# A convolution, scan and out-projection kernel on one core: five tiles per stream to begin with, masked taps on GpSimd, spare quarters on two banks

## The chip, the cores and the metric

The kernel runs on one core of a Trainium2 chip. The metric is the device time of one execution in microseconds, lower is better. Each execution that was profiled also has a span, from its first to its last instruction, which is 1.7 us shorter than its time (346.14 against 344.4). Below, "the trace" means the profiled execution, and "timed" all executions that a run lists. The profiled one is among these, except in the first run of before, where it took 346.14 us and is not among the four. No run is marked as in the chip's slower state (the single execution of before_look has no mark); "slow" below means longer than others of the same kernel.

## The reference, cut to what matters

```python
# x (8, 4224, 192), weight (8, 7): a causal convolution with one softmaxed row of 7 taps per head of 24 columns
out = np.einsum('hk,bskhg->bshg', w, x_unf)
# then a gated linear recurrence of 512 channels and a projection back to 192
proj = x @ w_in
val, gate = (proj[..., :D_inner], proj[..., D_inner:])
for t in range(S):
    h = a[0, 0] * h + val[:, t, :]
    ys[:, t, :] = h
silu = gate * (1.0 / (1.0 + np.exp(-gate)))
return (silu * ys @ w_out).astype(np.float32)
```

The rows of the eight sequences are taken as two streams of 16896. A stream is cut into tiles of 112 rows for the convolution and into 33 blocks of 512 for the rest. With four groups of 128 channels that makes 132 steps.

## The kernel before

TensorE (PE) does the convolution as matmuls with a banded matrix of taps (`tb`), transposes, projects, and projects back. A step is one `phase` (8 matmuls of 512 columns: the values of the next step, the gates of this one), two scans on VectorE (DVE), two silus on ScalarE (ACT), a product silu x scan on GpSimd (POOL), a part of the convolution of a later group, and two or three quarters of the out-projection. A quarter is 4 matmuls of 192 columns; two quarters fill half an output tile (a block of one stream), one PSUM bank, which ACT copies out. The 256 quarters are eight more than two for each of the 124 steps that take them; these eight are the "spare" ones.

```python
    def seam_taps(t):                      # where a tile holds the end of one sequence and the start of the next
        off = seams[t]
        if t not in tbs:
            tbs[t] = singles.tile([K, H, M], BF16, name=f"tb_{t}")
            nc.scalar.copy(tbs[t], tb)
        else:
            nc.scalar.memzero(tbs[t][0 : off + HB, :, off:M])
    # ... cut ...
            for k in range(2):             # of outp(): w counts the output tiles, k their halves
                ps = bank(k if w >= WL else 0)
                for b in (2 * k, 2 * k + 1):
                    outp_mm(ps, w, b, range(NC))
                    # ... cut: ACT copies after the second quarter, a store after the fourth ...
    # ... cut ...
    F = QT + QT // 2                       # six tiles of each stream are loaded, convolved and turned first
    # ... cut ...
    phase(-1)                              # the first projection
    second(FQ, QT, bank(0), bank(1), (nc.scalar, nc.scalar))   # what is left of the second four tiles
    WL = NOUT - 8
    for s in range(NSTEP):
        # ... cut: scan, phase, product, loads ...
        if 0 < gr <= len(seams) and o < 2:
            seam_taps(sorted(seams)[gr - 1])
        for k, n in enumerate(todo.get(s, [])):
            conv(n, 1 - k)                 # convolutions of later groups, on bank 1, until step 119
        if s >= 2 * LW:
            for _ in range(3 if s >= NSTEP - SPG and s % 2 == 0 or s == NSTEP - 1 else 2):
                next(out_quarters)
```

## Time and profile before

| | before |
|---|---|
| time, median of 4 runs (range) | 344.57 us (344.29 to 344.79) |
| time of the profiled execution | 346.14 us, span 344.4 us |
| PE, DVE, POOL, ACT busy | 96%, 94%, 90%, 74% |
| idle of PE behind the bank's copy | 4.9 us in 5 waits |

These are the busy shares of its page and two rows of its costliest groups (busy us, mean ns of one, then idle time of the engine before them and what ended most of it):

```profile
PE 329.0 (96%) x2605; PEld 179.1 (52%) x2608; DVE 324.4 (94%) x312; ACT 256.4 (74%) x525; POOL 309.9 (90%) x177
...
L425 PE MATMUL pm<-wout,y 128*128 128x192 bf16 x1040 | 107.3, 246 | 5.1 <-ACT osb L457 4.9
...
L255 ACT COPY tb<-tb 128x896 bf16<-128x896 bf16 x3 | 2.8, 940 | 0.0
```

The row of line 425 is the out-projection; its 5.1 us of idle PE are what the third part of the change aims at. Line 255 is the copy of the taps that the second part moves. The rows of a timeline further down give start and length in us, then engine, line, operation, tiles, shapes and count; a bracket holds the idle time of the engine before the row and what ended it.

### The profile page before, as it was taken

To read this page: it belongs to the slowest core of one execution; us is meant where nothing else is said; L and a number is where in the kernel's file an instruction comes from. 1 tells how busy PE (TensorE), PEld (TensorE's weight loads), DVE (VectorE), ACT (ScalarE), POOL (GpSimd) and SP (SyncE) were. 2 spreads that over 40 slices of the span, in tenths; PEclk is the share of its full clock that TensorE was granted. 3 is DMA by queue.
4 is the path that set the end of the run, shared out by engine and by line. 5 is a ranking of instruction groups with operands and counts; after the bars stand their busy time and mean duration, and the time that the engine had idled before them with its cause. 6 is when DMAs were issued, how large, how long until landed. Compare 5 with 4: busy or idle time off the path is not lost.

```text
span 344.4 us, 7246 instructions
## 1 busy us (share of the span) xinstructions
PE 329.0 (96%) x2605; PEld 179.1 (52%) x2608; DVE 324.4 (94%) x312; ACT 256.4 (74%) x525; POOL 309.9 (90%) x177
## 2 busy tenths in 40 slices
PE   6989999999999999999999999999999999969993
PEld 2533545555555555555555555555555555535553
DVE  4799999999999999999999999999999999967993
ACT  5777878778788887777877878777877877755662
POOL 8779999898999899989998999999999999856991
PEclk9999999999999999999999999999999999999998
DMA  8996999999799989978996999797969594442225
GB/s 152 159 135 99 148 184 200 200 144 187 141 196 143 212 141 188 161 192 133 191 166 191 149 195 177 170 133 193 158 190 147 137 176 131 104 116 93 91 93 185
DMA packets 124878, 54.28 MB, mean 158 GB/s; under 512 B 90758, under 2 KB 124522, under 8 KB 124842
## 3 DMA queue, kind: packets, MB, share of 16 engines
q1 hardware_dynamic: 85034, 38.21, 49.3%
q0 software_dynamic: 39424, 15.24, 40.4%
q8 instruction: 20, 0.33, 0.4%
q10 hardware_dynamic: 384, 0.37, 0.4%
q14 instruction: 16, 0.13, 0.2%
HBM read 31.04 MB, written 25.95 MB: 165 GB/s over the span
## 4 chain that ended last, share of the span: by engine, by line
PE 86%; DMA 5%; ACT 3%; DVE 3%; issue 2%; POOL 0%; DVEq 0%; ACTq 0%; POOLq 0%
PE pm L425 25%; PE pv L342 15%; PE pg L342 15%; PE pg L350 11%; PE pm L282 11%; PE pv L350 8%; DMA out_dram<-osb 3%; DVE h L396 2%; DMA xb<-in_x_dram 2%; ACT sg L378 1%; ACT osb L457 1%; ACT tb L255 0%; PE pg L425 0%; POOL xb L126 0%; ACT xc L527 0%
## 5 line engine op out<-in xcount | busy, mean ns | idle before, releaser
L396 DVE TENSOR_TENSOR_SCAN h<-av,h,pv 128x512 bf16<-128x512 f32 (+3 forms) x256 | 293.9, 1209 | 7.0 <-POOL y L414 4.7
L414 POOL TENSOR_TENSOR y<-sg,h 128x1024 bf16<-128x1024 bf16 x130 | 274.2, 2123 | 25.6 <-ACT sg L378 22.0
L378 ACT ACTIVATE sg<-pg 128x512 bf16<-128x512 f32 x262 | 142.2, 595 | 72.6 <-PE pg L350 68.4
L425 PE MATMUL pm<-wout,y 128*128 128x192 bf16 x1040 | 107.3, 246 | 5.1 <-ACT osb L457 4.9
L425 PEld LDWEIGHTS <-y 128*128 128x128 bf16 x1056 | 84.8, 98 | 17.3 <-issue 16.4
L342 PE MATMUL pv<-xc,w 128*128 128x512 bf16 x265 | 79.7, 379 | 1.6 <-DVE h L396 1.3
L342 PE MATMUL pg<-xc,w 128*128 128x512 bf16 x260 | 77.8, 379 | 0.6 <-ACT sg L378 0.4
L342 PEld LDWEIGHTS <-w 128*128 128x128 bf16 x528 | 49.3, 98 | 33.9 <-issue 3.8
L457 ACT COPY osb<-pm 128x384 f32<-128x384 f32 x128 | 63.4, 499 | 1.9 <-DMA out_dram<-osb 0.9
L282 PEld LDWEIGHTS <-tb 128*112 128x112 bf16 x438 | 33.2, 129 | 45.5 <-issue 45.3
L350 PE MATMUL pg<-xc,w 64*128 64x512 bf16 x262 | 51.0, 386 | 0.0
L350 PE MATMUL pv<-xc,w 64*128 64x512 bf16 x266 | 50.6, 376 | 0.0
L282 PE MATMUL pm<-xb,tb 128*112 128x192 bf16 (+7 forms) x419 | 48.7, 238 | 0.0
L350 PEld LDWEIGHTS <-w 64*128 64x128 bf16 x528 | 15.3, 94 | 57.0 <-issue 56.8
L112 ACT CAST ymain<-pm 112x512 bf16<-112x512 f32 x73 | 42.6, 589 | 0.4 <-PE pm L282 0.4
L126 POOL DMA_DIRECT2D xb<-in_x_dram x30 | 29.7, 1006 | 0.8 <-POOLq L614 0.8
L396 DVE TENSOR_TENSOR_SCAN h<-av,pv 128x512 bf16<-128x512 f32 (+3 forms) x32 | 25.2, 798 | 0.8 <-PE pv L350 0.8
L303 ACT CAST yquad<-pm 112x512 bf16<-112x512 f32 x36 | 21.2, 589 | 0.0
L176 PE MATMUL pg<-wm 128*128 128x512 bf16 x11 | 5.1, 629 | 1.7 <-DVE wm L169 1.7
L176 PEld LDWEIGHTS <-wm 128*128 128x128 bf16 x14 | 1.5, 127 | 3.8 <-issue 1.9
L114 DVE CAST ymain<-pg 112x512 bf16<-112x512 f32 x1 | 0.7, 690 | 2.3 <-PE pg L282 2.3
L255 ACT COPY tb<-tb 128x896 bf16<-128x896 bf16 x3 | 2.8, 940 | 0.0
(70 smaller groups left out, 39.6 us busy)
## 6 DMA issues: line engine op xcount, KB each, us to landing
out_dram<-osb SPq DMA_DIRECT2D x65, 384.0 KB, 3.0
xb<-in_x_dram POOLq DMA_DIRECT2D x12, 768.0 KB, 8.8
xb<-in_x_dram POOLq DMA_DIRECT2D x9, 384.0 KB, 9.7
xc<-ymain SPq DMA_TRANSPOSE x70, 4.1
xb<-in_x_dram POOLq DMA_DIRECT2D x4, 192.0 KB, 6.6
xc<-yquad SPq DMA_TRANSPOSE x35, 3.2
xraw<-in_x_dram SPq DMA_DIRECT2D x2, 192.0 KB, 4.3
xb<-in_x_dram POOLq DMA_DIRECT2D x2, 144.0 KB, 5.9
```

The source lines that it names most:

```text
L112: eng.copy(o, i)
L126: eng.dma_start(t[:, b0:n, :], dataclasses.replace(xf, offset=xf.offset + (row + b0 * M) * D, ap=[[D, K], [M * D, n - b0], [1, D]],),)
L176: nc.tensor.matmul(ps, wm[:, 0:P], wm, start=True, stop=True)
L282: nc.tensor.matmul(pc[:, :, t0 - a0 : t1 - a0, lo - lo0 : hi - lo0], tap[:, h, :], xbs[g][:, :, a + t0 : a + t1, lo:hi], start=(lo == lo0) ...
L303: nc.scalar.copy(y.rearrange("p t d -> p (t d)"), ps[0:M, :])
L342: nc.tensor.matmul(ps[st], w1[:, m * P : (m + 1) * P], xc[:, st, t], start=True, stop=False)
L350: nc.tensor.matmul(ps[st], w2[r, m * P : (m + 1) * P], xc[r, 2, t], start=False, stop=True)
L378: nc.scalar.activation(sg[:, st * N : st * N + N], pgs[st], Act.Silu)
L396: nc.vector.tensor_tensor_scan(h[:, o + lo : o + hi], av[:, c : c + 1].to_broadcast([P, hi - lo]), pv[st][:, lo:hi], initial=0.0 if lo in ...
L414: eng.tensor_mul(y, sg, h)
L425: nc.tensor.matmul(bank[:, b % 2 * D : b % 2 * D + D], y[:, b : N : NB] if w >= NOUT - 2 else y[:, b * P : b * P + P], wout[:, c, :], star ...
L457: nc.scalar.copy(osb[:, 2 * k : 2 * k + 2, :].rearrange("p b d -> p (b d)"), ps[:, 0 : 2 * D],)
```

## The change

Its intent is in three parts. (1) Begin with five tiles of each stream instead of six, so that the first projection has less to wait for. (2) Make the three masked copies of the taps on GpSimd before its first product, instead of on ACT in the middle of the steps. (3) Spread the eight spare quarters of the out-projection so that none comes while convolutions still hold bank 1, and alternate the banks from then on.

```diff
-    F = QT + QT // 2
-    assert F * M >= N
+    F = -(-N // M)
+    assert F == QT + 1
...
-    def seam_taps(t):
-        ... (cut, shown above)
+    for t, off in seams.items():
+        tbs[t] = singles.tile([K, H, M], BF16, name=f"tb_{t}")
+        nc.gpsimd.tensor_copy(tbs[t], tb)
+        nc.gpsimd.memset(tbs[t][0 : off + HB, :, off:M], 0.0)
...
-    second(0, FQ, p1[0], p2[0], (nc.vector, nc.scalar))
+    second(p1[0], 0, 1, 0, D1, nc.vector)
+    second(p2[0], 0, 1, D1, D, nc.scalar)
...
     phase(-1)
-    second(FQ, QT, bank(0), bank(1), (nc.scalar, nc.scalar))
+    second(ps_g.tile([P, N], FP32, name="pg_0"), 1, QT, D1, D, nc.scalar)
+    for k in range(2):
+        second(bank(k), 1, QT, k * D2R, k * D2R + D2R, nc.scalar)
     out_quarters = outp()
-    WL = NOUT - 8
+    WL = NOUT - 10
+    spare = [NSTEP - 12 + 2 * k for k in range(6)] + [NSTEP - 3, NSTEP - 1]
...
-        if 0 < gr <= len(seams) and o < 2:
-            seam_taps(sorted(seams)[gr - 1])
...
-            for _ in range(3 if s >= NSTEP - SPG and s % 2 == 0 or s == NSTEP - 1 else 2):
+            for _ in range(3 if s in spare else 2):
```

The body of `second` is rewritten for one piece at a time (cut here).

More of the change, by code (lines that the diff above doesn't have):

```diff
@@ L248 @@
     tbs = {}
-    def seam_taps(t):
-        off = seams[t]
-        if t not in tbs:
-            tbs[t] = singles.tile([K, H, M], BF16, name=f"tb_{t}")
-            nc.scalar.copy(tbs[t], tb)
-        else:
-            nc.scalar.memzero(tbs[t][0 : off + HB, :, off:M])
+    for t, off in seams.items():
+        tbs[t] = singles.tile([K, H, M], BF16, name=f"tb_{t}")
+        nc.gpsimd.tensor_copy(tbs[t], tb)
+        nc.gpsimd.memset(tbs[t][0 : off + HB, :, off:M], 0.0)
     one = singles.tile([NC, NC], FP32, name="one")
@@ L476 @@
     p2 = [ps_v.tile([P, n], FP32, name=f"pv_{k}") for k, n in enumerate((N, NC))]
-    tiles = lambda p, d: p[0:M, :].rearrange("p (s a d) -> p s a d", d=d, s=2)
     mixed = lambda p: p[0:M, :].rearrange("p (a s d) -> p s a d", s=2, a=QT)
@@ L483, with second @@
     nc.scalar.copy(ymix[0][:, 0:QT, :], p1[1][0:M, :].rearrange("p (t d) -> p t d", d=P))
-    FQ = F - QT
-    def second(a0, a1, pa, pb, eng):
-        taps(tiles(pa, P), 1, 0, P, a0, a1)
-        taps(mixed(pb)[:, :, a0:a1, :], 1, D1, D, a0, a1)
-        copy(eng[0], y1[:, :, a0:a1, :], tiles(pa, P))
-        copy(
-            eng[1], ymix[0][:, QT + a0 : QT + a1, :],
-            pb[0:M, :].rearrange("p (t d) -> p t d", d=P)[:, a0:a1, :],
-        )
-    second(0, FQ, p1[0], p2[0], (nc.vector, nc.scalar))
+    m1 = ymix[0].rearrange("p t (s d) -> p s t d", s=2)[:, :, QT : HT, :]
+    def second(ps, a0, a1, lo, hi, eng):
+        pc = ps[0:M, 0 : 2 * (a1 - a0) * (hi - lo)].rearrange(
+            "p (s a d) -> p s a d", s=2, a=a1 - a0
+        )
+        taps(pc, 1, lo, hi, a0, a1)
+        to = m1[:, :, a0:a1, :] if lo == D1 else y1[:, :, a0:a1, lo:hi]
+        copy(eng, to, pc)
+    second(p1[0], 0, 1, 0, D1, nc.vector)
+    second(p2[0], 0, 1, D1, D, nc.scalar)
     av = singles.tile([P, NC], FP32, name="av")
```

## The prediction

> **What bounds the kernel now.** I read the page's busy shares first. TensorE (PE) is busy 96% of 344.4 us, VectorE (DVE) 94%, GpSimd (POOL) 90%, ScalarE (ACT) 74%. So I did not look for a busy engine but for the idle time of PE, and asked for PE's waits stretch by stretch. Of the whole span after the start:
>
> ```profile
> PE pm L425 <- ACT osb L457: 4.9, 5, 1.2
> PE pv L342 <- DVE h L396: 1.3, 5, 0.4
> ```
>
> (us in total, times, the longest.) Line 425 is the out-projection, line 457 the copy that empties its PSUM bank, line 396 the scan. Of the first row the last 45 us alone hold:
>
> ```profile
> PE pm L425 <- ACT osb L457: 3.9, 4, 1.2
> ```
>
> The timeline of that stretch shows the four:
>
> ```profile
> 302.46 0.49 PE L425 MATMUL pm<-wout,y 128*128 128x192 bf16 x4 [0.82 <-ACT osb L457]
> ...
> 306.22 0.49 PE L425 MATMUL pm<-wout,y 128*128 128x192 bf16 x4 [1.18 <-ACT osb L457]
> ...
> 309.78 0.82 PE L425 MATMUL pm<-wout,y 128*128 128x192 bf16 x8 [1.23 <-ACT osb L457]
> ...
> 315.55 0.49 PE L425 MATMUL pm<-wout,y 128*128 128x192 bf16 x4 [0.62 <-ACT osb L457]
> ```
>
> Each is a step where a quarter starts a new half tile while the one bank (pm_0) still waits for ACT, which does two silus (1.08 us) before the copy. Last, the chain that ended last, for the start:
>
> ```profile
> 1.32 0.95 POOL xb L126
> 2.27 5.80 DMA xb<-in_x_dram
> 8.21 0.65 PE pg L282 x7
> ...
> 11.87 0.59 PE pv L342 x2
> 12.46 0.44 PE pv L350 x2
> ...
> 23.55 1.55 DVE h L396 x2
> ```
>
> Three regimes follow. To 12.8 us the chain is load, convolution, transposes, first projection. From 12.8 to 33 us it is the scans: single scans start 1.171 us apart, so 2.34 us a step. From 33 us on it is PE: 2.42 us in a step with a convolution, 2.17 without (out-projection at 84.40 to 86.61, 151.87 to 154.04), and from 52.3 to 300.8 PE is busy 248.40 of 248.50 us. There only an idle PE can be won. Its waits after 33.2 us are one of 1.10 at 52.24, two of 0.05 at 86.61 and 120.19, and the four above.
>
> **What the Trainium skill says.** "PSUM — Partial Sum Buffer", Summary: rules for kernel authors, says to read PSUM while matmuls run from a different bank than the one written. The trace agrees: where quarters already alternate (after 317 us) no such wait is left. "GPSIMD Engine Reference", 3.1 Elementwise, gives about 2.6 cycles an element with two inputs, and 4.1 Engine selection says one input is roughly line rate. The trace agrees on the first: 1024 elements take 2.12 us, 2.07 ns each, some 2.5 cycles of the page's 1.2 GHz. No GpSimd copy is in this trace to test the second. "DMA: Bandwidth & Descriptors", Issuing engines are not separate DMA queues, says that all issuers share the same 16 engines and interleave. The trace agrees: output stores land 3.0 us after issue in the median, but the first, issued at 41.15 among loads and transposes, took 10.46.
>
> **Part 1: five tiles instead of six.** The raw float loads shrink from two tiles to one per stream (tile 0 comes apart), 512 packets of 768 B to 256. Until 6.5 us they share the engines with the GpSimd loads that the chain waits for. At about 50 ns a packet, as both kinds show, 256 packets over 16 engines are 0.8 us; I count 0.6 us off the landing at 8.07. The first transposes fall from 18 to 15 (0.058 us apart), the ACT copy of 672 columns (0.72 us) becomes one of 560 (about 0.62), the two DVE copies of 0.50 become about 0.44: together 0.2 us before the first projection. So the first scan starts about 0.8 us earlier, at 12.0.
>
> Part of that is paid back. What is left of the second quad is three tiles, not two: three ACT copies of 384 columns (0.50 each by the row of osb) in place of 0.58 and 0.38, nine transposes in place of six, and a DVE copy of 1008 columns in place of 672 (0.51, about 0.68). The transposes wait for the third ACT copy, so scan 1 comes about 0.45 us later after scan 0 than now. The DVE has 0.8 us of gaps before scans 2 and 3 (0.26 and 0.55), set by the chain of PE and ACT, which itself moves by some 0.3. Net at scan 3: 0.8 - 0.3 = 0.5 us earlier, and the scans then run back to back as now.
>
> **Part 2: masked taps on GpSimd.** ACT loses three copies of 128x896 (0.94 us each) and three zeroings (0.31 to 0.51): 4.05 us of ACT, but in the chain only where PE waits after them, at 86.61 and 120.19: 0.05 us each, 0.10 in all. At 52.24 ACT had finished its copy (49.82 to 50.76) and then waited 0.95 us for a store, so nothing is won there. GpSimd gains three copies and three memsets behind its ten load issues, which end at 13.5 us. Estimate from the skill's line rate and 1.2 GHz: 896 elements 0.75 us plus about 0.1 (its 1-element memset takes 0.10), up to 1.4 if slower; memsets of 256, 512 and 768 elements at the 1 ns an element of the 112-element memset (0.21 us), 0.3 to 0.9. Sum about 4.8 us, so the first product starts at 18.4 instead of 15.9. But GpSimd idles 1.78 us before the second product (19.79), and that one comes at about 20.5: a lag of 0.7 us that lasts while GpSimd is back to back, to about 53 us. Products have slack: that of step 3 ends at 26.9, its reader runs at 34.8; six buffers hold the silus. It costs nothing by itself, but the four loads of the third group (30.98 to 40.07) go out 0.7 us later.
>
> **Part 3: spare quarters.** The old spare quarter at step 118 (300.98) shifts the pairing and gives the waits at steps 118, 119, 120 and 122. Now steps 118 and 119, the last with convolutions on bank 1, take two quarters; from step 120 banks alternate, and of the 8 spare quarters 6 fall on even steps and 2 on steps 129 and 131. No step touches a bank twice across a copy. All four waits go: 0.82 + 1.18 + 1.23 + 0.62 = 3.85 us. PE has the same matmuls otherwise. Could DVE take over? Steps 119 to 129 hold 26.1 us of PE work by the pieces of the chain (1.40 a phase, 0.77 or 1.10 of quarters, 0.36 of convolution), 2.37 a step, against 2.34 for two scans: PE still sets it, barely. Its products hold: that of step 127 ends 4.8 us after the phase of 127 begins (phase 1.40, silu 1.2, product 2.2), and its first reader, the second quarter of step 129, comes some 6.4 us after (steps of 2.17 and 2.50, a phase of 1.40, one quarter of 0.33).
>
> **The join at 52 us.** Between the start and the PE regime lies the wait of 1.10 us, for a store that landed at 51.61. If its landing is fixed by the DMA traffic, arriving 0.5 us earlier only waits longer, and loads issued 0.7 us later may push it back. I give 3 in 4 that it stays, with PE resuming about 0.2 us later than now, and 1 in 4 that it vanishes and both it and the start's 0.5 are won: 0.75 x 0.2 - 0.25 x 1.6 = -0.25 us.
>
> Sum: -3.85 - 0.10 - 0.25 = -4.2 us, 344.4 to 340.2 us.
>
> **Rivals.** (a) The GpSimd work delays products and loads: if copies run at the two-input rate (1.9 us each, sum 8 us), the lag is near 3 us, the store at 52 lands later, and the total is about 342. For it: GpSimd has no idle time from 20 to 53 us; against it: products have over 7 us of slack. (b) The scan takes the place of the removed waits: DVE stood 4.69 us idle in the same stretch, so it has what it needs; if it were behind by a pair it would return at most 1 us: 341.2. (c) The store at 52 us lands early and the whole start counts: 344.4 - 3.85 - 0.1 - 1.1 - 0.5 to 1.0, 338.4 to 338.9. (d) The start gains nothing, as the load's last packets sit behind the projection weights' 2 KB packets: with the join holding, no change to the total.
>
> **Range and chances.** The end is counted from four measured waits, so the spread is nearly all that of the join, -1.6 to +1.2 us. 8 in 10: 338.9 to 341.6. Over 2% faster needs under about 337.6, more than all gains together: 4%. Slower by 2% would need a new stall of over 10 us: 1%.
>
> **What would show it.** In the changed profile: no wait of PE for line 457 after 300 us; quarters three to a step on 128 to 131; the first convolution near 7.6 and the first scan near 12.0 us; GpSimd copies from about 13.6 us, with the first product near 18.4; a single wait of PE near 52 us, of 1 to 2.3 us. Wrong would be: waits of scans for GpSimd, silus waiting for products, or gaps of PE behind the scan from step 120 on.

## More of the kernel before

Differences of the whole kernel are given between times, differences inside it between traces, and the two are not mixed without saying so.

Before the first convolution PE runs "warming" matmuls on zeros, `warm(pw, WARM)` with 7 and `warm(pw, WARM2)` with 4, as its clock begins at half speed: the first of them, of 512 columns, start 0.43 us apart, and matmuls of this size after the rise of the clock 0.22.

## The result, and the profile after

The changed kernel took 340.2 us in the median of 4 runs (339.2 to 341.54), before 344.57. The ratio is 0.9876, with a 95% interval of 0.9841 to 0.9911: 1.2% faster. A ratio is the mean time of one kernel's fast runs over that of the other's of the same rounds, so it is not quite the ratio of the medians that are quoted.

The page after, the rows that answer to those of before (the lines are renumbered: 421 is the old 425, 453 the old 457, 338 and 346 the old 342 and 350):

```profile
PE 327.9 (97%) x2608; PEld 178.9 (53%) x2609; DVE 323.7 (96%) x312; ACT 253.3 (75%) x520; POOL 313.8 (93%) x183
...
L421 PE MATMUL pm<-wout,y 128*128 128x192 bf16 x1040 | 106.7, 246 | 0.0
...
L253 POOL COPY tb<-tb 128x896 bf16<-128x896 bf16 x3 | 2.9, 952 | 0.0
```

The out-projection has no idle time left before it, and GpSimd has the copies. All waits of PE in the changed kernel (us in total, times, longest):

```profile
PE pg L176 <- DVE wm L169: 1.7, 1, 1.7
PE pv L338 <- DVE h L392: 1.3, 5, 0.4
PE pg L338 <- ACT sg L374: 0.4, 1, 0.4
PE pm L278 <- DMA xb<-in_x_dram: 0.3, 1, 0.3
PE pv L338 <- ACT xc L112: 0.2, 1, 0.2
```

The row "PE pm <- ACT osb" of 4.9 us is gone, and all that is left lies before 32 us. The timeline of PE at steps 119 to 121, where there had been waits of about a microsecond:

```profile
300.68 0.82 PE L421 MATMUL pm<-wout,y 128*128 128x192 bf16 x8
...
302.83 1.17 PE L421 MATMUL pm<-wout,y 128*128 128x192 bf16 x12
...
305.33 0.83 PE L421 MATMUL pm<-wout,y 128*128 128x192 bf16 x8
```

Rows of 8, 12 and 8 matmuls without a bracket: two, three and two quarters, with no wait before or within. The start of the chain that ended last:

```profile
5.63 2.27 POOL xb L126 x3
7.89 6.21 DMA xb<-in_x_dram
14.24 0.65 PE pm L278 x7
```

The chain of before waited at 8.21 us for the first loads. This one goes back, from the third group of four tiles at 14.24, to loads that GpSimd issued until 7.89: the beginning has moved in front of its data. And GpSimd's masks, by the timeline:

```profile
13.56 1.01 POOL L253 COPY tb<-tb 128x896 bf16<-128x896 bf16 x1
14.62 0.31 POOL L254 MEMSET tb<- 96x256 bf16 x1
...
17.31 0.73 POOL L254 MEMSET tb<- 32x768 bf16 x1
18.01 2.11 POOL L410 TENSOR_TENSOR y<-sg,h 128x1024 bf16<-128x1024 bf16 x1
```

They take from 13.56 to 18.01, 4.45 us, and the first product follows at once.

Between the two traces the scans run 1.20 us earlier from step 3 on, 2.56 us from step 52 on, and the last matmul ends 7.01 us earlier (339.20 and 332.19). The timed medians differ by only 4.4. The rest is the choice of executions: that of before was 1.6 us slower than its median, that of after 1.0 faster.

### The profile page after: what moved, and what is told of

It reads as the page before. It is cut to its first block, busy times and chain, and to the rows that moved or that the text cites. A ratio compares the mean times of both kernels' runs of the same rounds, so it can differ in the third digit from the quotient of the medians.

```text
span 337.5 us, 7251 instructions
## 1 busy us (share of the span) xinstructions
PE 327.9 (97%) x2608; PEld 178.9 (53%) x2609; DVE 323.7 (96%) x312; ACT 253.3 (75%) x520; POOL 313.8 (93%) x183
## 4 chain that ended last, share of the span: by engine, by line
PE 90%; DVE 3%; POOL 2%; DMA 2%; issue 1%; ACT 1%; DVEq 0%; POOLq 0%
PE pm L421 26%; PE pg L338 16%; PE pv L338 16%; PE pg L346 12%; PE pm L278 11%; PE pv L346 8%; DVE h L392 2%; DMA xb<-in_x_dram 2%; POOL xb L126 1%; PE pg L421 0%; ACT sg L374 0%; ACT xc L522 0%; DVE osb L114 0%; POOL w L202 0%; POOL w L201 0%
## 5 line engine op out<-in xcount | busy, mean ns | idle before, releaser
L278 PE MATMUL pm<-xb,tb 128*112 128x192 bf16 (+6 forms) x417 | 48.5, 238 | 0.3 <-DMA xb<-in_x_dram 0.3
L112 ACT CAST ymain<-pm 112x512 bf16<-112x512 f32 (+1 forms) x74 | 42.9, 586 | 0.5 <-PE pm L278 0.5
L253 POOL COPY tb<-tb 128x896 bf16<-128x896 bf16 x3 | 2.9, 952 | 0.0
L414 POOL TENSOR_TENSOR y<-sg,h 128x512 bf16<-128x512 bf16 x2 | 2.3, 1149 | 0.0
```

What stands on the lines that cost most here:

```text
L112: eng.copy(o, i)
L278: nc.tensor.matmul(pc[:, :, t0 - a0 : t1 - a0, lo - lo0 : hi - lo0], tap[:, h, :], xbs[g][:, :, a + t0 : a + t1, lo:hi], start=(lo == lo0) ...
```

## The experiments

**The change once more (again).** No edit.

> The changed kernel once more, as the yardstick for the three runs beside it. Its four earlier times lay between 339.2 and 341.54 us, against 344.29 to 344.79 of before, and its profile came from the fastest of them, while the profile of before came from an execution of 346.14. Theory: the times spread because the wait near 52 us for a store comes and goes; then the new trace shows either no wait of PE there and about 339 us, or one of 1 to 2 us and about 340.5. Rival: the spread is the granted clock (0.995 in the slowest, 0.999 in the fastest); then slow and fast executions differ by a lower clock in their records and not by a wait at 52 us.

Measured: 339.70 us (339.58 to 339.86), before 344.20, ratio 0.9864. The trace has no wait of PE after 33 us, and its profiled execution took 339.86, as the timed ones. Its first convolution began at 7.19 us, that of the first trace of after at 6.65: neither the wait at 52 us nor a lower clock later on makes the difference (in both, the clock falls only after the last matmul), but the start: scan 3 is at 20.62 instead of 20.11 and the last matmul ends 0.50 us later. More on that below.

**Without part 3 (no_part3).**

```diff
-    WL = NOUT - 10
-    spare = [NSTEP - 12 + 2 * k for k in range(6)] + [NSTEP - 3, NSTEP - 1]
+    WL = NOUT - 8
...
-            for _ in range(3 if s in spare else 2):
+            for _ in range(3 if s >= NSTEP - SPG and s % 2 == 0 or s == NSTEP - 1 else 2):
```

> The changed kernel with the old spare quarters and the old switch to two banks (part 3 undone). Theory: each of the four waits costs its shown idle time and besides the 0.16 us by which the last matmul before it is drawn longer (0.246) than matmuls follow one another (0.083): 3.85 + 4 x 0.16 = 4.5 us slower than the unchanged after of this round. Prediction as on record: 3.85 us. Rival: the scans would have limited the end anyway; then under 3.5 us.

Measured: 343.85 us, 4.15 slower than the change beside it. Nearly all of the gain sits here. (The two pieces of part 3, the steps of the spare quarters and the earlier use of two banks, were not run apart.) PE's waits from 290 us on, and two of the four in its timeline:

```profile
PE pm L421 <- ACT osb L453: 3.6, 4, 1.2
```

```profile
299.28 0.25 PE L421 MATMUL pm<-wout,y 128*128 128x192 bf16 x1
300.36 0.49 PE L421 MATMUL pm<-wout,y 128*128 128x192 bf16 x4 [0.83 <-ACT osb L453]
...
302.44 0.49 PE L421 MATMUL pm<-wout,y 128*128 128x192 bf16 x4
304.12 0.49 PE L421 MATMUL pm<-wout,y 128*128 128x192 bf16 x4 [1.18 <-ACT osb L453]
```

Here the true cost of a wait can be read. Four matmuls are drawn as 0.49 us from 302.44, but where matmuls follow on, the next begins 0.33 us after the first of the four. The last one is drawn 0.246 us long, while the next would have started after 0.083. So between the start of the last one and the next start there is a slot of 0.083 in a stream, and 0.246 + idle at a wait: each wait costs its idle and some 0.16 us. From first matmul to first matmul, the four out-projections with a wait took 1.978, 2.001, 2.109 and 1.779 us, where 12, 8, 12 and 12 such matmuls without one take 1.001, 0.660, 1.001 and 1.001. That is 4.20 us in all, against 3.58 of idle time shown (0.827 + 1.182 + 0.949 + 0.618). The Trainium skill, "TensorE: Matmul & The Clock Gate", Single matmul latency, gives (398 + N)/2.4 ns for one matmul, an estimate of 246 ns for 192 columns, and its section Back-to-back issue gap gives N/2.4 + 2.5, an estimate of 82.5 ns, which the page limits to matmuls without weight loads between. Only the second can be tested by this trace: starts lie 82 or 83 ns apart, here with a weight load for each matmul. The drawn 246 ns tests nothing, as the profile models the ends of matmuls. What tests the 0.16 us is the loss by starts: 3.58 + 4 x 0.16 is 4.2 us, as measured.

**Without part 2 (no_part2).**

```diff
-        nc.gpsimd.tensor_copy(tbs[t], tb)
-        nc.gpsimd.memset(tbs[t][0 : off + HB, :, off:M], 0.0)
+            nc.scalar.copy(tbs[t], tb)                                # in seam_taps, at the first of two steps
+            nc.scalar.memzero(tbs[t][0 : off + HB, :, off:M])         # at the second
```

> The changed kernel with the masked taps made by ScalarE again, at the steps where they were (part 2 undone). Theory: two bubbles of 0.05 + 0.16 us come back near 84 and 118 us, 0.4 us in all, and a third near 51 us if PE is not waiting for a store there anyway. Prediction as on record: 0.1 us. Rival: the 4.5 us of GpSimd work at the start delays the loads of the third group and costs something at 52 us; then this run is no slower or even faster than after, with loads issued earlier.

Measured: 340.27 us, 0.57 slower than the change, but with a spread of 339.20 to 342.78. Its trace has a bubble in PE at 50.30, 84.68 and 118.26 (its lines are numbered five higher than those of the change). The second, with the same step of the change (again) beside it:

```profile
84.25 0.38 PE L351 MATMUL pv<-xc,w 64*128 64x512 bf16 x2
84.68 0.82 PE L426 MATMUL pm<-wout,y 128*128 128x192 bf16 x8
```

```profile
84.34 0.38 PE L346 MATMUL pv<-xc,w 64*128 64x512 bf16 x2
84.65 0.83 PE L421 MATMUL pm<-wout,y 128*128 128x192 bf16 x8
```

From row to row 0.43 us against 0.31, and 0.01 comes back within the eight matmuls: 0.107 us each, 0.32 for the three. The trace shows 0.05 us of idle before each. So the bubbles cost less than the 0.21 of the theory and twice what the idle shows. The rival is out: GpSimd's loads went out earlier in this run (its first product at 14.67 instead of 18.05), and nothing was won by that.

**Without part 1 (no_part1).** The kernel before with parts 2 and 3.

```diff
-    F = -(-N // M)
-    assert F == QT + 1
+    F = QT + QT // 2
+    assert F * M >= N
... (second() and its calls as before)
```

> The changed kernel begun from six tiles per stream again (part 1 undone; parts 2 and 3 kept). Theory: the start is worth the 1.2 us by which scan 3 moved in the two traces, and it reaches the end except for what a store at 52 us eats: 0.5 to 1.2 us slower than after in the same state of that wait. Prediction as on record: 0.5 us at scan 3 and, with the store fixed by DMA traffic, nothing at the end. Rival: all of it is eaten at 52 us, 0 us.

Measured: 339.21 us (339.13 to 339.34), 0.49 faster than the whole change (339.58 to 339.86). The sign is the other way round from all that was expected. The timeline of PE at the start, first of the change (again), then of this run:

```profile
5.20 1.89 PE L176 MATMUL pg<-wm 128*128 128x512 bf16 x4
7.19 0.65 PE L278 MATMUL pg<-xb,tb 128*112 128x192 bf16 x7
```

```profile
5.20 1.53 PE L176 MATMUL pg<-wm 128*128 128x512 bf16 x4
7.16 0.65 PE L278 MATMUL pg<-xb,tb 128*112 128x192 bf16 x7 [0.42 <-DMA xb<-in_x_dram]
```

With five tiles the data had landed at 6.54 us, but the first convolution stood in PE's queue behind four warming matmuls, which ran at half speed (0.43 us from start to start): by the records the clock rose at 7.15 us in this execution, at 6.25 in the other and at 5.85 in the first trace of after. With six tiles the data landed at 7.03, and the matmuls were ahead of it. Both began to convolve at the same moment, and five tiles then have the longer rest of the second four tiles before scan 1.

**The kernel before, looked at again (before_look).** No edit, one look.

> The kernel before, for a second trace. Its first trace is of an execution of 346.14 us, where the others took 343.8 to 344.8. Theory: that execution was an unlucky one: loads late by about 1 us (first convolution at 8.21) and a store late at 51.61 (PE idle 1.10 there). Then this trace has its first convolution near 7.2, as the run with six tiles and parts 2 and 3 had, no long wait of PE near 50 us, and a time near 344.2. Rival: both belong to the kernel before; then they are here again.

Measured: 345.74 us, where the timed runs of before took 344.05 to 345.57. The first convolution was at 7.66, between theory and rival. The waits of PE behind the bank's copy:

```profile
PE pm L425 <- ACT osb L457: 4.8, 5, 1.2
```

Five again, the one near 50 us with 0.94. So that wait belongs to the kernel before in both of its traces, though both were of slow executions.

**Six tiles and four store buffers (six_o4).** The kernel without part 1, and:

```diff
-    o_pool = ctx.enter_context(tc.tile_pool(name="op", bufs=3))
+    o_pool = ctx.enter_context(tc.tile_pool(name="op", bufs=4))
```

> Six tiles with parts 2 and 3, as in the run without part 1, and four store buffers instead of three, so that no copy waits for a store near 50 us. Theory: without part 1 the kernel was at 339.21 against 339.70, because five tiles cost 0.5 us between scans 0 and 3; this one is again 0.3 to 0.6 us faster than the five-tile kernel with four buffers beside it. Rival: the 0.5 us were luck of the start or of the store near 50 us; then the two are within 0.2 us.

**The change and four store buffers (five_o4).** The same edit.

> The changed kernel with four store buffers instead of three. Theory: the store near 50 us lands within some tenths of its need, and in some executions late; with a fourth buffer that wait can't be, so the slow executions of after (341.54) vanish and the median is at or a little under 339.7. Rival: the spread comes from the start alone (the TensorE clock rises at 4.7 to 7.2 us); then median and spread stay as they are.

Measured: 339.56 us (339.40 to 340.86) and 340.21 us (339.04 to 341.89). In the median six tiles are again faster, by 0.65, but this time the ranges overlap. The slow executions do not vanish with the fourth buffer, so the spread of the five-tile kernel does not come from the stores. The trace of five_o4 shows what happens when its clock rises early and the first convolution begins at 6.72:

```profile
10.74 0.51 PE L346 MATMUL pv<-xc,w 64*128 64x512 bf16 x2
11.67 0.35 PE L278 MATMUL pg<-xb,tb 128*112 128x96 bf16 x3 [0.42 <-DMA xb<-in_x_dram]
```

PE waits 0.42 us for the loads of tiles 5 to 7, which landed at 11.54.

**Fewer warming matmuls (less_warm).**

```diff
-WARM2 = 4
+WARM2 = 2
```

> The changed kernel with two instead of four warming matmuls after the taps. In the trace of the repeated run the data had landed at 6.54, but the first convolution started at 7.19, behind the warming matmuls, as the clock rose only at 7.15. Theory: what the five-tile start waits for now is the warming; with two fewer the first convolution starts at about 6.5 us in every execution and scan 3 comes up to 0.6 us earlier, 0.3 us in the median time. Rival: the clock then rises later and the convolutions and transposes run slow; same time or slower.

Measured: 341.97 us (340.39 to 343.35), 1.8 to 2.3 slower than the change (340.21 with four buffers, 339.70). The first convolution did begin early, at 6.75. The stretches of PE from 6 to 20 us (length, PE busy, instructions, granted clock, DMA share, GB/s), first of this run, then of the change (again):

```profile
6.00:9.70 3.70, 3.04 (x36) 1.00 1.13 153
9.70:13.20 3.50, 2.35 (x21) 1.00 1.43 158
13.20:16.60 3.40, 3.22 (x18) 0.50 1.58 188
16.60:20.00 3.40, 3.40 (x28) 1.00 1.60 193
```

```profile
9.70:13.20 3.50, 3.21 (x32) 1.00 1.35 144
13.20:16.60 3.40, 3.31 (x29) 1.00 1.56 183
```

After a stretch in which PE was busy 2.35 of 3.50 us, as it waited for weights and tiles (0.26 us at 11.47, 0.67 us at 12.52), the granted clock was 0.5 for 3.41 us, and scan 1 came 2.2 us later than in the run again (17.05 and 14.84). The Trainium skill, "TensorE: Matmul & The Clock Gate", What's actually happening, says that the clock is set by PE's activity in free-running windows of 3413 ns; the length agrees with the record. But the drawn busy share does not tell when the clock falls. In less_warm the 3.41 us before the fall, from 9.76 us, hold 2.26 us of busy PE. Two stretches of the same length, of before and of before_look, hold as little, each from the rise of the clock on, and it did not fall after them:

```profile
7.02:10.43 3.41, 2.27 (x24) 1.00 1.22 162
5.49:8.90 3.41, 2.11 (x23) 1.00 1.30 202
```

**The stretch filled (less_warm_filled).**

```diff
-WARM2 = 4
+WARM2 = 2
...
     phase(-1)
+    warm(bank(0), 3)
     second(ps_g.tile([P, N], FP32, name="pg_0"), 1, QT, D1, D, nc.scalar)
```

> Five tiles, two warming matmuls fewer before the convolution as in the run less_warm (341.97), and three warming matmuls put back behind the first projection, where PE waited for loads. In less_warm the granted clock was 0.5 for 3.4 us from 13.18 us, after a stretch in which PE had waited. Theory: a stretch with too little PE work makes the clock fall; with the stretch filled it does not fall, and the time goes back to 340 or under. Rival: the fall comes from elsewhere (the missing warming itself); then it stays near 342.

Measured: 339.91 us in the median, four executions at 339.56 to 340.07 and two at 342.65 and 343.66. So filling the stretch brings most executions back, as the theory has it, though that the clock stayed up in these is inferred from their times: no trace shows one. The trace is of the slowest: there the clock rose only at 14.51 us, the convolutions and transposes before it ran slow, and scan 1 came at 17.90. In this execution the two missing warming matmuls thus had a price of their own; both the theory and its rival hold a part.

**Four store buffers in the kernel before (before_o4).** The edit of six_o4 alone.

> The kernel before with four store buffers instead of three, nothing else. Both traces of before show PE idle for 0.94 and 1.10 us near 51 us behind a store, but both traced executions (346.14, 345.74) were slower than the timed ones beside them (344.0 to 345.6). Theory A: the wait is in the timed executions too; then this kernel is about 1.1 us faster than before. Theory B: it comes only when the profiler writes along; then the times are equal within 0.3 us, and the profiled execution alone gains.

Measured: 343.83 us (343.76 to 344.06), before 344.44 (343.97 to 347.36). The gain of 0.6 lies between the two theories: the fastest executions of before are as fast, the slow ones are gone. So the wait for the store seems to be in some timed executions and not in others; the interval of the ratio, 0.9938 to 1.0001, leaves room for no gain at all. In the trace the wait is not there, but the first store landed at 48.52 us, early enough for three buffers too, so this trace does not test the fourth.

**Part 3 alone (only_part3).** The edit of no_part3 the other way round, in the kernel before.

> The kernel before with part 3 alone (quarters and banks). Theory: the four waits of the end go, 3.85 us shown plus 4 x 0.16, so 4.3 us (by the run without part 3, 4.15) in the ratio to before: near 0.9878. Rival: the parts help each other and this one alone gives clearly less than 4.15.

Measured: 339.93 us, 4.51 less than before beside it, ratio 0.9857. Part 3 needs no help from the others.

**Six tiles once more (six_again).** The kernel of no_part1.

> Parts 2 and 3 without part 1 (six tiles), timed once more, with three store buffers. Theory: it was at 0.985 of before where the whole change was at 0.9864 beside it, and is again at 0.985 to 0.9865, that is not slower than the whole change. Rival: the first timing was lucky; then 0.988 or more.

Measured: 339.30 us, ratio 0.9858, four executions at 339.0 to 339.5 and two at 341.13 and 341.76. Against only_part3 beside it part 2 is worth 0.63 in the median, but only 0.07 in the mean (339.92 and 339.99), because of its two long executions. In the median this is the fastest kernel, twice, but only by half a microsecond.

## Why the prediction was right

The time was right, 340.2 us, but in part by luck, as terms missed in opposite directions: parts 3 and 2 gave 4.15 and 0.57 us in the times instead of 3.85 and 0.10, and the five tiles lost 0.49 where the start and the join were to gain 0.25 together. By its own steps:

**The four waits of the end.** The mechanism was right: single bank, spare quarter at the wrong step, copy behind two silus; all four are gone in every trace that has part 3. The size was too small: 3.85 us was the sum of the idle times shown. By starts of matmuls the four cost 4.48 us in both traces of before and 4.20 in those of no_part3 and before_o4, and 4.15 and 4.51 in the times of two rounds. The term that was mis-sized is the drawn length of the last matmul before a wait, 0.16 us each. Scans did not take over: in the run again the only trace of them at the end is one projection that took 0.04 us longer than the others (at 306.5 us).

**The masked taps.** The prediction gave 0.10 us, from two idles of 0.05, and left out the third bubble, as it lay hidden under the wait for a store. Measured are three of 0.107 us, 0.32 in all, and 0.57 and 0.63 between the medians of the times (0.76 and 0.07 between their means), whose spread does not allow to tell these apart from 0.32. GpSimd behaved as worked out: 4.45 us for copies and memsets instead of 4.8 (the terms of the prediction itself, three copies of 0.85 and 0.3, 0.6 and 0.9 for the memsets, add up to 4.4), the first product at 18.01 instead of 18.4, the second at 20.10, loads of the third group issued from 31.30 instead of 30.98. A copy took 0.92 to 1.01 us for 896 elements, 1.03 to 1.12 ns each against 2.07 for the product with two inputs, so "GPSIMD Engine Reference", 4.1 Engine selection (one input is roughly line rate), holds here. That it costs nothing was right. (Of its two examples of a step of 2.17 us the first, 84.40 to 86.61, is 2.21 long, as it holds one of the bubbles.)

**The five tiles.** First convolution, first scan and scan 3 of all twelve traces at the start, without the two runs with fewer warming matmuls:

| us | first convolution | scan 0 | scan 3 | scan 0 to 3 |
|---|---|---|---|---|
| six tiles, mean of 7 traces | 7.45 | 12.06 | 20.56 | 8.50 in each |
| five tiles, mean of 5 traces | 6.84 | 11.29 | 20.45 | 8.92 to 9.53 |

The first scan comes 0.77 us earlier in these means, 0.58 without the two slow traces of before. The prediction had 0.8, but counted from the slow trace: it named 7.6 and 12.0 us for the first convolution and scan, and the five traces have 6.45 to 7.20 and 10.90 to 11.65. The step that failed is "Part of that is paid back ... some 0.3": 0.67 us on average are paid back. Scan 1 does come 0.42 to 0.48 us later after scan 0, as worked out (0.45), in the three traces without a wait for loads before it. But the gaps before scans 2 and 3 take up nothing of it: scan 3 starts 5.77 us after scan 1 with six tiles (all seven traces) and with five (four of five; in the first of after 5.87, where PE waited 0.3 us for loads of the third four tiles). And in the two other traces PE, begun early, waits for the loads of the tiles that it needs next (0.42 and 0.57 us), and scan 1 is 0.89 and 1.03 us later; this wait was not in the prediction.

Net at scan 3 the table shows a gain of 0.1 us instead of 0.5, and the times a loss of 0.49 and 0.65 us in two rounds. Most of this contradiction is the choice of traces. From the start of scan 3 to the end of the last matmul the traces with parts 2 and 3 took 312.03 us with six tiles (three traces) and 312.03 to 312.07 with five (three), so part 1 changes nothing after scan 3. Without the two slow traces of before, six tiles have scan 3 at 20.37 us, 0.09 earlier than five. And the traces of five tiles flatter: those of after and five_o4 are of executions 1.0 and 0.8 us faster than the medians of their runs, where the five of six tiles that are left lie within 0.2 of theirs. So the loss of half a microsecond very likely lies before scan 3 in the slower executions with five tiles. What holds these up is open, as none of them has a trace. The pair of traces whose executions were typical of their kernels (339.27 and 339.86) shows a loss of 0.35 us at scan 3, with the clock's rise at 7.15 us (five tiles) and 6.25 (six).

**The join near 52 us.** The prediction gave 3 in 4 that the wait for the store stays. It was in neither trace of after. In the twelve traces of the table the first store lands at 47.4 to 51.6 us, and PE stands before the bank at 50 to 51. Three of the traces lost time there (1.10, 0.94 and 0.51 us of idle), all of kernels without parts 1 and 2; the fourth of that kind, with four buffers, did not. So this step failed as well. Timed, the wait is worth up to 0.6 us of before. Which part moved the store is not settled.

Together, from times: part 3 4.15, part 2 0.57, part 1 -0.49: 4.2 us, against 4.5 between the medians; the wait for the store has room in the remaining 0.3.

## What to carry to other kernels

Count a stall of TensorE from the start of the last matmul before it to the start of the next one, and take off the distance that they have in a stream; the idle time drawn is too small by what the drawn length of a matmul exceeds that distance (here 0.16 us). Before reading small waits from a trace, see whether its execution is a typical one: here two of the terms were of an execution 1.6 us slower than the median, and the traces of the change were mostly of executions faster than theirs. A start made shorter on one side runs into the next thing that it needs, here the next tiles and the clock, so test such a part alone.

## What the Trainium skill lacked or had wrong

- "TensorE: Matmul & The Clock Gate", Single matmul latency and Back-to-back issue gap: the page does not say that idle time read between drawn matmuls understates a stall, about by the difference of its two formulas (0.16 us at 192 columns): 3.58 us shown in four waits, 4.20 lost.
- The same page, The HAM clock gate: its table has the clock fall after an idle window, and no figure says how little work within a window is too little. Here it fell to 0.5 for 3.41 us after 3.41 us in which PE was busy 2.26, and stayed up after two others with 2.27 and 2.11.
- The same page says that the rise varies by 500 ns either way from run to run. In the traces with all warming matmuls the record of full clock begins between 4.73 and 7.20 us, though the first warming matmul begins at 1.65 to 1.67 in all; with two fewer it began at 14.51 in one of two.
- "GPSIMD Engine Reference": no figure for a memset. Here 256, 512 and 768 elements of bf16 per partition took 0.31, 0.52 and 0.73 us.
- "DMA: Bandwidth & Descriptors": no figure for a store behind loads and transposes. The first store here took 7.5 to 10.5 us from issue to landing, against a median of 3.0 to 3.8.
